# Attention, Fourier mixing and a two-layer network in one kernel: new token groups, weight sums moved from GpSimd to VectorE, buffers kept double for one more batch

## The chip, the cores and the metric

The kernel runs on one core of one Trainium2 chip. The metric is the device time of one execution in microseconds (us); the time of a kernel is the median over its runs. The engines are called by the names of the profile: PE is TensorE (matrix products; PEld its weight loads), DVE is VectorE, ACT is ScalarE, POOL is GpSimd, SP is SyncE, which here only issues DMAs. Each engine works its own instructions strictly in the order in which they stand, and waits on semaphores for the others.

## What is computed

For 8 batches of 448 tokens, 12 heads of 64:

```python
scores = scale * np.matmul(q, k.transpose(0, 1, 3, 2))
attn = np.maximum(scores, 0.0) ** 2 / S
x = attn @ v                                   # heads side by side: 768 channels
mixed = np.real(np.fft.fft(np.fft.fft(x, axis=1), axis=2))
u = x + mixed                                  # over tokens, then over channels
un = (u - mean(u)) / np.sqrt(var(u) + 1e-6)    # per token
out = u + np.maximum(un @ w_ch1, 0.0) @ w_ch2  # 768 -> 3072 -> 768
```

Attention and the Fourier mixing need a whole batch. The two layers of the network work on any token by itself.

## The kernel before, in words

**Batches and groups.** Attention and mixing go by batch, b = 0 to 7. The network goes by groups of tokens that run across batch borders; `GT` (L171) holds the borders. There are nine groups, called 0 to 8 here: 384, 512, 256, 512, 512, 512, 256, 512 and 128 tokens.

**A batch.** `load_group` (L305) fetches q, k and v of four heads at a time from POOL; three such loads make a batch. q and k have two buffers each, of which `home` (L301) picks one: both are used in turn up to load 10, from load 11 on only one. `turning` (L400) copies q and k on DVE (L412) and transposes them by DMA from SP (L424). `attention` (L525) computes scores on PE (L588, three pieces of a head pair at a time), takes relu on ACT (L612) and squares on DVE (L618) into one of nine buffers `sq` (six from batch 3 on), and multiplies by v on PE (L573). `fold` (L465) scales the result, and forms sums and differences for the Fourier step on DVE (L474 to L511). `mix` (L1019) does the channel transform on PE (L1035), `mix_rows` (L858) the token transform (L866), then adds x on POOL and DVE into `u` (L886, L888), computes mean and variance (L901), and writes the normalised rows `un` on POOL (L918). u and un go to DRAM (L940 from SP, L943 from POOL as an indirect store). `u` and `un` have two sets of buffers up to batch 2, and one from batch 3 on (`side`, L629; L906 and L916): with one set the second half of the rows waits until the first half is stored.

**A group.** `turn_un` (L966) transposes a group's rows from DRAM into the tile `unT` by DMA from SP (L972). It waits for the stores of un and for a free unT buffer: there are two, `unT0` and `unT1`, but `unT0` is given up after group 0 to hold weight sums, so all later groups share `unT1`. `ffn` (L1177) then does the first layer (L1222, 144 products whatever the group's size, as wide as the group), relu on ACT (L1200), and the second layer. Groups in `PLAIN` (0, 1 and 8) do the second layer with 24 products for each 128 tokens and half of the 768 channels (L1255). All others take two blocks of 128 tokens as a `Pair` (L1265) and use Strassen's scheme on 16 of the 24 hidden blocks: 88 products (L1312) where the plain way has 96, with extra sums of relu outputs on DVE (L1293 to L1305) and with sums of `w_ch2`'s blocks. Each product's result is added to u on DVE (L1209) and stored (L1168).

**The weight sums.** `weight_sums` (L1093) makes four sets of eight blocks, 128 partitions x 384, once, on POOL (L1104): T3, T2, T4 and T1. They are put into tiles that are free by then: `unT0`, `uA` and `u1A`, two `sq` and `qn0`, `kn0`. T1 overwrites a block of w_ch2 in place, once group 1, a plain one, has read it (`w2_free`). Group 8, plain again, needs that block, so `load_left` (L1119) loads it a second time at the end of attention.

**Who sets the order.** The engines' programs are written out by a planner (`Streams`, L63). Each part of the work is a stream that asks for an engine with an estimated duration, dependences and buffers; the planner always takes the request that can start first, and so fixes the order of the instructions on every engine. A wrong estimate makes an engine wait with work behind it. Attention is held back so that it stays ahead of the network by a fixed amount: PE may take the next scores of batch b when the network's progress, in batches, has reached b plus the batch's share done minus `LEAD` (L1396, L559).

Of the kernel before, what the change touches and what calls it, by code (L numbers as in the profile page):

```python
# [142 lines left out]
def kernel(  # L143
# [9 lines left out]
    nc = tc.nc  # L153
# [17 lines left out]
    GT = [0, 384, 896, 1152, 1664, 2176, 2688, 2944, 3456, B * S]  # L171
# [129 lines left out]
    def home(i):  # L301

        return (i - NG) % 2 if i < 4 * NG - 1 else 1
# [96 lines left out]
    def turning():  # L400

        for b in range(B):
            for g in range(NG):
# [5 lines left out]
                for x in range(2):  # L409
# [115 lines left out]
    def attention(b):  # L525
# [3 lines left out]
        if b == 3:  # L529
# [3 lines left out]
        room = NSQ if b < 3 else NSQ - 3  # L533
# [95 lines left out]
    def side(b, ch):  # L629

        return ch if b < 3 else 1
# [226 lines left out]
    def mix_rows(b, ch, pcs):  # L858
# [47 lines left out]
        e = yield need("DVE", 0.3, [e3 + LATENCY["ACT"]], [BUN[ch if b < 3 else 0]])  # L906
# [5 lines left out]
        for i, u in enumerate(us):  # L912
# [3 lines left out]
            un = work.tile([128, D], BF16, name="un", tag=f"un{2 * (ch if b < 3 else 0) + i}", bufs=1)  # L916
# [164 lines left out]
    PLAIN = (0, 1, NGR - 1)  # L1081
# [3 lines left out]
    sums, left, left_ready = [Cell() for _ in range(5)], [], Cell()  # L1085
    ffn_begun = [Cell() for _ in range(NGR)]
    unt_left, w2_free, attended = Cell(), Cell(), Cell()
# [5 lines left out]
    def weight_sums():  # L1093

        def slots(tag, count, deps):
            yield need("POOL", 0.0, deps)
            t = work.tile([128, count, DH], BF16, name="wsum", tag=tag, bufs=1)
            return [t[:, i] for i in range(count)]

        def each(n, outs, xs, ys, op, deps):  # L1100
            T[n] = outs
            for i in range(KP):
                e = yield need("POOL", 1.3, deps)
                nc.gpsimd.tensor_tensor(outs[i], xs[i], ys[i], op=op)  # L1104
            sums[n].t = e + LATENCY["POOL"]

        t3 = yield from slots("unT0", 8, [unt_left] + w2_ready)
        b11, b12, b21, b22 = ([w2(2 * i + k, hf) for i in range(KP)] for k in range(2) for hf in range(2))
        yield from each(3, t3, b22, b12, ALU.subtract, [])
        t2 = yield from slots("uA", 4, u_left)  # L1110
        t2 += yield from slots("u1A", 4, u_left)
        yield from each(2, t2, t3, b11, ALU.add, [sums[3]])
        t4 = []
        for tag, dep in ((f"sq{NSQ - 2}", sq_left), (f"sq{NSQ - 1}", sq_left), ("qn0", qk_left), ("kn0", qk_left)):
            t4 += yield from slots(tag, 2, [dep])
        yield from each(4, t4, b21, t2, ALU.subtract, [sums[2]])
        yield from each(1, b12, b12, b11, ALU.subtract, [w2_free, sums[3]])

    def load_left():  # L1119

        yield need("POOL", 0.0, [attended])
        for i in range(0, KP, 2):
            e = yield need("POOL", 0.85)
            t = work.tile([128, 2, DH], BF16, name="left", tag=f"sq{i // 2}", bufs=1)
            nc.gpsimd.dma_start(out=t, in_=moe_w_ch2[2 * i * 128:(2 * i + 4) * 128, DH:D].rearrange(
                "(j p) d -> p j d", p=128)[:, 0::2])
            left.extend([t[:, 0], t[:, 1]])
        left_ready.t = sch.dma(e, KP * 128 * DH * 4, 360e3, "sw")
# [48 lines left out]
    def ffn(b):  # L1177
# [38 lines left out]
        for j in range(0, JC, JN):  # L1216
            hf, jj = divmod(j, JC // 2)
            e = yield need("PE", 6 * JN * mm(N), [w1_ready[hf]], [BF])
# [14 lines left out]
        if b == 0:  # L1233
# [12 lines left out]
        for c in range(NC):  # L1246
            for hf in range(2):
                for jq in range(4):
                    e = yield need("PE", 6 * mm(DH), ht[6 * jq:6 * jq + 6] + [w2_ready[jq]]
# [197 lines left out]
```

## Time and profile before

| what | value |
|---|---|
| median of three runs | 627.71 us (625.6 to 630.43) |
| the profiled execution | 628.35 us, of which the span of the trace 626.6 us |
| PE busy | 591.0 us (94%), 4118 products |
| DVE busy | 401.7 us (64%) |
| ACT busy | 293.2 us (47%) |
| POOL busy | 188.2 us (30%) |
| first layer, L1222, 512 wide | 165.9 us busy, 720 products |
| second layer, L1312 and L1255 | 1264 products of 384 columns |
| POOL weight sums, L1104 | 32 instructions, the four sets between 89.8 and 225.2 us |

A row of the timeline gives start, duration, engine, line, operation, output<-input, shape and count; in brackets stands the idle time of the engine before it and what ended it. Products overlap in the array, so the mean duration of one (387 ns at 512 columns) is longer than the step from one to the next: 24 of them in 5.29 us make a step of 220 ns. Steps, not durations, are what a chain of products costs. A row of windows gives busy time of each engine in a stretch of the span, and the clock that PE was granted there (1.00 is full).

### The profile page before, as it was taken

The numbers are of one execution on the slowest core, as the hardware profiler recorded it, in microseconds if no ns is written. First come the engines' busy times: TensorE is split into PE (matmuls) and PEld (weight loads), VectorE is DVE, ScalarE is ACT, GpSimd is POOL, SyncE is SP. The second block draws the span as 40 slices with busy tenths as digits, with TensorE's granted clock in tenths as the row PEclk, the third lists the DMA queues.
The fourth block names the chain that finished last, engine by engine and source line by source line (L and its number), as shares of the span: only waits on it lengthen the run. The fifth ranks groups of instructions, "written<-read, shape, count | busy, mean of one in ns | idle before, by whom it ended". The sixth has DMA issues, their size and how long they took to land.

```text
span 626.6 us, 10716 instructions
## 1 busy us (share of the span) xinstructions
PE 591.0 (94%) x4118; PEld 331.3 (53%) x4118; DVE 401.7 (64%) x886; ACT 293.2 (47%) x427; POOL 188.2 (30%) x236
## 2 busy tenths in 40 slices
PE   8999999899999989579999999999999999699997
PEld 6565556544544566224555454554545577344675
DVE  6977787846599867726598565975687759101520
ACT  5867741767344325338523556345572442044001
POOL 8442227111389535201243015121161016100000
PEclk9999999999999889979999999999999999899999
DMA  9999999768859764756957985598445364600220
GB/s 130 208 207 229 217 183 179 148 78 146 141 152 174 129 118 135 124 78 91 158 168 144 134 122 156 137 191 139 103 137 126 66 128 143 167 22 0 79 86 26
DMA packets 134484, 83.04 MB, mean 133 GB/s; under 512 B 77473, under 2 KB 129601, under 8 KB 134433
## 3 DMA queue, kind: packets, MB, share of 16 engines
q0 software_dynamic: 41408, 34.86, 35.0%
q1 hardware_dynamic: 93024, 47.50, 33.6%
q8 instruction: 32, 0.52, 0.3%
q14 instruction: 20, 0.16, 0.1%
HBM read 64.49 MB, written 26.69 MB: 146 GB/s over the span
## 4 chain that ended last, share of the span: by engine, by line
PE 71%; issue 10%; DVE 9%; DMA 3%; ACT 3%; POOL 2%; SPq 1%; POOLq 0%; DVEq 0%; ACTq 0%
PE psF L1222 33%; PE psF L1312 16%; PE psF L1255 7%; PE psF L573 5%; PE psS L588 5%; DVE sq L618 3%; DMA unT<-nbot 2%; PE psS L1035 2%; ACT sq L612 2%; PE psS L866 1%; SPq L972 1%; DVE o L1209 1%; DMA out_dram<-o 1%; DVE fold L497 1%; PE psS L665 1%
## 5 line engine op out<-in xcount | busy, mean ns | idle before, releaser
L1222 PE MATMUL psF<-unT,w 128*128 128x512 bf16 (+3 forms) x1296 | 231.9, 336 | 17.6 <-DMA unT<-nbot 15.8
L612 ACT ACTIVATE sq<-psS 112x896 bf16<-112x896 f32 x192 | 164.4, 916 | 115.4 <-PE psS L588 115.2
L1222 PEld LDWEIGHTS <-w 128*128 128x128 bf16 x1296 | 118.7, 99 | 121.8 <-issue 17.9
L1200 ACT ACTIVATE hT<-psF 128x512 bf16<-128x512 f32 (+1 forms) x162 | 95.5, 590 | 152.0 <-PE psF L1222 150.8
L618 DVE TENSOR_TENSOR sq<-sq 112x896 bf16<-112x896 bf16 x192 | 131.4, 699 | 35.5 <-ACT sq L612 34.5
L1312 PE MATMUL psF<-w,hT 128*128 128x384 bf16 x560 | 96.0, 326 | 0.0
L1312 PEld LDWEIGHTS <-hT 128*128 128x128 bf16 x720 | 69.6, 98 | 49.1 <-issue 3.7
L1209 DVE TENSOR_TENSOR o<-psF,o 128x384 f32<-128x384 f32 x96 | 53.0, 552 | 65.7 <-PE psF L1312 50.3
L1255 PE MATMUL psF<-w,hT 128*128 128x384 bf16 x376 | 66.2, 329 | 0.5 <-DVE o L1209 0.5
L588 PE MATMUL psS<-qkT 64*112 64x448 bf16 x384 | 52.9, 369 | 2.1 <-ACT sq L612 0.9
L319 POOL DMA_DIRECT2D vn<-in_v_dram x24 | 17.2, 718 | 118.7 <-PE psF L573 99.1
L1255 PEld LDWEIGHTS <-hT 128*128 128x128 bf16 x384 | 36.7, 98 | 28.1 <-issue 5.3
L573 PE MATMUL psF<-sq,vn 112*64 112x448 bf16 x384 | 46.4, 360 | 4.5 <-DVE o L1209 2.3
L474 DVE TENSOR_SCALAR xT<-psF 128x224 bf16<-128x224 f32 x48 | 18.7, 389 | 43.1 <-PE psF L573 42.9
L918 POOL TENSOR_SCALAR un<-u,rstd,nmr 128x768 bf16<-128x768 f32 (+1 forms) x24 | 28.3, 1186 | 54.4 <-DVE nmr L910 54.3
L588 PEld LDWEIGHTS <-qkT 64*112 64x112 bf16 x384 | 20.9, 126 | 27.8 <-issue 21.6
L573 PEld LDWEIGHTS <-vn 112*64 112x64 bf16 x384 | 18.3, 109 | 27.9 <-issue 19.6
L1293 DVE TENSOR_TENSOR s<-hT 128x768 bf16<-128x768 bf16 (+1 forms) x20 | 8.8, 438 | 33.3 <-ACT hT L1200 32.6
L1312 PE MATMUL psF<-wsum,hT 128*128 128x384 bf16 x160 | 29.3, 326 | 0.1
L901 DVE BATCH_NORM_STATS2 stats<-u 128x6 f32<-128x384 f32 (+1 forms) x56 | 28.4, 540 | 0.0
L319 POOL DMA_DIRECT2D qn<-in_q_dram x21 | 15.1, 717 | 44.0 <-DVE qkr L412 36.2
L943 POOL DMA_INDIRECT ubot<-u,back x16 | 16.7, 1046 | 24.0 <-ACT hT L1200 19.8
(139 smaller groups left out, 542.0 us busy)
## 6 DMA issues: line engine op xcount, KB each, us to landing
out_dram<-o SPq DMA_DIRECT2D x56, 192.0 KB, 1.9
vn<-in_v_dram POOLq DMA_DIRECT2D x24, 224.0 KB, 4.9
qn<-in_q_dram POOLq DMA_DIRECT2D x21, 224.0 KB, 4.9
kn<-in_k_dram POOLq DMA_DIRECT2D x21, 224.0 KB, 5.6
w<-in_moe_w_ch_dram POOLq DMA_DIRECT2D x12, 384.0 KB, 13.5
w<-in_moe_w_ch_dram POOLq DMA_DIRECT2D x4, 1152.0 KB, 22.6
utop<-u SPq DMA_DIRECT2D x8, 384.0 KB, 2.7
o<-utop SPq DMA_DIRECT2D x16, 192.0 KB, 4.2
```

Of the source, the lines that this page charges most:

```text
L319: nc.gpsimd.dma_start(out=t, in_=src[b, hs].rearrange("h (p j) d -> p h (j d)", j=4))
L573: nc.tensor.matmul(av[h * Dh:(h + 1) * Dh, 0:S], lhsT=vn[:, c, h0 + h, :], rhs=sq[:, h, :], start=(c == 0), stop=(c == 3))
L588: nc.tensor.matmul(sc[:R, h, 0:S].rearrange("k (c q) -> k c q", c=4), lhsT=kT[ps, m % 2, c, :], rhs=qT[ps, m % 2], start=True, stop=True)
L612: nc.scalar.activation(r, sc[:R, :, 0:S], AF.Relu)
L618: nc.vector.tensor_tensor(r, r, r, op=ALU.mult)
L901: nc.vector.bn_stats(stats[:n, hf, :], u[:n, hf * (D // 2):(hf + 1) * (D // 2)])
L918: nc.gpsimd.tensor_scalar(un[:n], u[:n], rstd[:n, i:i + 1], nmr[:n, i:i + 1], op0=ALU.mult, op1=ALU.add)
L1200: nc.scalar.activation(hs, ps, AF.Relu)
L1209: nc.vector.tensor_tensor(o, pc[:, 0:DH], o, op=ALU.add)
L1222: nc.tensor.matmul(ph[:, i * N:(i + 1) * N], lhsT=w1_sb[m][hf][:, (jj + i) * 128:(jj + i + 1) * 128], rhs=unT[:, m, 0:N], start=(m == 0), ...
L1255: nc.tensor.matmul(pc[:, 0:DH], lhsT=h[:, j, c * 128:(c + 1) * 128], rhs=left[j // 2] if swap else w2(j, hf), start=(j == 0), stop=(j == J ...
L1312: nc.tensor.matmul(pc[:, 0:n], lhsT=lhs[i], rhs=rhs[i], start=(start and i == 0), stop=(i == k - 1), skip_group_check=True)
```

## The change

- The groups become 384, 512, 384, 512, 256, 512, 512 and 512 tokens: eight, called 0 to 7. Plain are 0, 1 and 2; the nine pairs of groups 3 to 7 use the seven products.
- Group 2 is transposed into `unT0`, so groups 1 and 2 have a buffer each; `unT0` is given up to the sums after group 2's first layer.
- The weight sums go from POOL to DVE, up to three blocks in one instruction (15 instructions), and T1 is made after group 2. The second load of w_ch2's block and its stream go.
- q/k buffers stay double up to load 11, and `u`, `un` and the nine `sq` buffers up to batch 3, one batch longer.
- `LEAD` goes from 2.3 to 2.6 batches.

```diff
-    GT = [0, 384, 896, 1152, 1664, 2176, 2688, 2944, 3456, B * S]
+    GT = [0, 384, 896, 1280, 1792, 2048, 2560, 3072, B * S]
...
-        return (i - NG) % 2 if i < 4 * NG - 1 else 1
+        return (i - NG) % 2 if i < 4 * NG else 1
...
-                    if b * NG + g != 4 * NG - 3:
+                    if b * NG + g != 4 * NG - 1:
                         BQ[x][home(b * NG + g)].free.append(e)
...
-        if b == 3:
+        if b == 4:
             yield need("ACT", 0.0, [], [BSQ] * 3)
...
-        room = NSQ if b < 3 else NSQ - 3
+        room = NSQ if b < 4 else NSQ - 3
...
-        attended.t = max(t for t, _ in sq_ids)
...
-        return ch if b < 3 else 1
+        return ch if b < 4 else 1
...
-        e = yield need("DVE", 0.3, [e3 + LATENCY["ACT"]], [BUN[ch if b < 3 else 0]])
+        e = yield need("DVE", 0.3, [e3 + LATENCY["ACT"]], [BUN[ch if b < 4 else 0]])
...
-            un = work.tile([128, D], BF16, name="un", tag=f"un{2 * (ch if b < 3 else 0) + i}", bufs=1)
+            un = work.tile([128, D], BF16, name="un", tag=f"un{2 * (ch if b < 4 else 0) + i}", bufs=1)
...
-            if b == 2 and ch == 0:
+            if b == 3 and ch == 0:
                 u_left[i].t = t
...
-            if b == 2 and ch == 1:
+            if b == 3 and ch == 1:
                 un_left.t = n_stored[b][3].t
             else:
-                BUN[0].free.append(n_stored[b][2 * ch + 1].t)
+                BUN[ch if b < 3 else 0].free.append(n_stored[b][2 * ch + 1].t)
...
-                g = work.tile([128, MC, 512], BF16, name="unT", tag="unT1", bufs=1)
+                g = work.tile([128, MC, 512], BF16, name="unT", tag=f"unT{int(len(groups) != 2)}", bufs=1)
...
-    PLAIN = (0, 1, NGR - 1)
+    PLAIN = (0, 1, 2)
...
-        def each(n, outs, xs, ys, op, deps):
-            T[n] = outs
-            for i in range(KP):
-                e = yield need("POOL", 1.3, deps)
-                nc.gpsimd.tensor_tensor(outs[i], xs[i], ys[i], op=op)
-            sums[n].t = e + LATENCY["POOL"]
...
+        def several(n, outs, x, y, op, deps):
+
+            def blocks(z, i0, i1):
+                if isinstance(z, tuple):
+                    k, hf = z
+                    j0 = 2 * i0 + k
+                    return w2_sb[j0 // 6][:, j0 % 6:j0 % 6 + 2 * (i1 - i0) - 1:2, hf * DH:(hf + 1) * DH]
+                return z[i0][0][:, z[i0][1]:z[i0][1] + i1 - i0]
+
+            i0 = 0
+            for i1 in range(1, KP + 1):
+                whole = [z for z in (outs, x, y) if not isinstance(z, tuple)]
+                if i1 < KP and i1 % 3 and all(z[i1][0] is z[i0][0] for z in whole):
+                    continue
+                e = yield need("DVE", dve2((i1 - i0) * DH), deps)
+                a, b, c = (blocks(z, i0, i1) for z in (outs, x, y))
+                nc.vector.tensor_tensor(a, b, c, op=op)
+                i0 = i1
...
+            sums[n].t = e + LATENCY["DVE"]
...
+        yield from several(3, t3, b22, b12, ALU.subtract, [])
...
+        yield from several(2, t2, t3, b11, ALU.add, [])
...
+        yield from several(4, t4, b21, t2, ALU.subtract, [])
+        yield from several(1, b12, b12, b11, ALU.subtract, [w2_free])
-
-    def load_left():
-
-        yield need("POOL", 0.0, [attended])
-        for i in range(0, KP, 2):
-            e = yield need("POOL", 0.85)
-            t = work.tile([128, 2, DH], BF16, name="left", tag=f"sq{i // 2}", bufs=1)
-            nc.gpsimd.dma_start(out=t, in_=moe_w_ch2[2 * i * 128:(2 * i + 4) * 128, DH:D].rearrange(
...
-        if b == 0:
+        if b == 2:
             unt_left.t = e
...
-        if b == 1:
+        if b == 2:
             w2_free.t = e + LATENCY["PE"]
...
-    LEAD = 2.3
+    LEAD = 2.6
...
-        sch.add(load_left(), (6, 6))
```

More of the change, by code (lines that the diff above doesn't have):

```diff
@@ L1084 @@
     T = [None] * 5
-    sums, left, left_ready = [Cell() for _ in range(5)], [], Cell()
+    sums = [Cell() for _ in range(5)]
     ffn_begun = [Cell() for _ in range(NGR)]
-    unt_left, w2_free, attended = Cell(), Cell(), Cell()
+    unt_left, w2_free = Cell(), Cell()
     def w2(j, hf):
@@ L1093, in weight_sums, with home @@
     def weight_sums():
-        def slots(tag, count, deps):
-            yield need("POOL", 0.0, deps)
+        def home(tag, count, deps):
+            yield need("DVE", 0.0, deps)
             t = work.tile([128, count, DH], BF16, name="wsum", tag=tag, bufs=1)
-            return [t[:, i] for i in range(count)]
-        def each(n, outs, xs, ys, op, deps):
-            T[n] = outs
-            for i in range(KP):
-                e = yield need("POOL", 1.3, deps)
-                nc.gpsimd.tensor_tensor(outs[i], xs[i], ys[i], op=op)
-            sums[n].t = e + LATENCY["POOL"]
@@ L1107, in weight_sums @@
[L1107 to L1112, printed above, removed]
+            return [(t, i) for i in range(count)]
+        def several(n, outs, x, y, op, deps):
[14 more added lines that the diff above has]
+                i0 = i1
+            T[n] = [w2(2 * i + outs[0], outs[1]) if isinstance(outs, tuple) else outs[i][0][:, outs[i][1]]
+                    for i in range(KP)]
+            sums[n].t = e + LATENCY["DVE"]
@@ L1116, in weight_sums @@
[L1116 to L1128 removed]
+            t4 += yield from home(tag, 2, [dep])
```

14 lines of the change are left out of this document (7 added, 7 removed).

## The prediction

> **What bounds the kernel now.** I read the page's slices first, then the waits, then the chain of work that ended last, then the timeline around each gap of PE. Groups and batches are counted from 0.
>
> The slices say that PE is the bound nearly everywhere, so only its gaps and its clock can be won:
>
> ```profile
> PE   8999999899999989579999999999999999699997
> PEclk9999999999999889979999999999999999899999
> ```
>
> A slice is 15.7 us. The digits 5, 7 and 6 in PE's row, and the 8s in the clock's row, are three places: 204 to 235, 251 to 282 and 533 to 548 us. The waits (who waited for what: total, times, longest) name two causes:
>
> ```profile
> PE psF L1222 <- DMA unT<-nbot: 15.8, 3, 10.4
> ...
> PE psS L1035 <- DVE fold L511: 2.9, 1, 2.9
> ...
> PE psF L573 <- DVE o L1209: 2.3, 1, 2.3
> ```
>
> The timeline of PE has them in place, the idle time in brackets:
>
> ```profile
> 182.77 0.38 PE L573 MATMUL psF<-sq,vn 112*64 112x448 bf16 x2 [1.00 <-DVE sq L618]
> 184.31 3.08 PE L1255 MATMUL psF<-w,hT 128*128 128x384 bf16 x18 [0.45 <-DVE o L1209]
> 204.94 1.19 PE L573 MATMUL psF<-sq,vn 112*64 112x448 bf16 x8 [2.34 <-DVE o L1209]
> 226.45 0.34 PE L1035 MATMUL psS<-chan,fold 128*128 128x193 bf16 x1 [2.88 <-DVE fold L511]
> 270.87 5.48 PE L1222 MATMUL psF<-unT,w 128*128 128x512 bf16 x18 [10.35 <-DMA unT<-nbot]
> 350.57 1.46 PE L1222 MATMUL psF<-unT,w 128*128 128x512 bf16 x6 [0.53 <-DMA unT<-nbot]
> 544.24 34.20 PE L1222 MATMUL psF<-unT,w 128*128 128x512 bf16 x144 [4.97 <-DMA unT<-nbot]
> ```
>
> Three of these wait for a group's transposed rows (groups 3, 4 and 7). The first four wait for DVE, and the timeline of DVE and POOL around the third shows what held it:
>
> ```profile
> 197.08 5.90 DVE L618 TENSOR_TENSOR sq<-sq 112x896 bf16<-112x896 bf16 x1
> 197.25 5.24 POOL L1104 TENSOR_TENSOR wsum<-w,wsum 128x384 bf16<-128x384 bf16 x6
> ...
> 203.09 0.61 DVE L618 TENSOR_TENSOR sq<-sq 112x896 bf16<-112x896 bf16 x1
> ```
>
> The same square takes 0.61 us alone and 5.90 us while six of POOL's weight sums run. A fold at 221.45 takes 3.90 us beside four sums (221.70, 3.50 us). So a run of POOL's sums holds DVE, and PE behind it.
>
> A gap costs more than its length. In the windows of 2 us (PE busy first, then PEld, DVE, ACT, POOL, granted clock, DMA share, GB/s) the clock is half for some time after it:
>
> ```profile
> 206.00:208.00 2.00, 2.00 (x11) 0.79 (x10) 1.02 (x3) 1.28 (x2) 1.56 (x2) 0.50 0.89 173
> 272.00:274.00 2.00, 2.00 (x6) 0.70 (x5) 0.00 (x0) 0.29 (x1) 0.00 (x0) 0.56 0.03 3
> 548.00:550.00 2.00, 2.00 (x6) 0.73 (x5) 0.00 (x0) 0.45 (x1) 0.00 (x0) 0.50 0.62 176
> ```
>
> The chain gives the step of a product, and what the half clock cost (start, duration, count):
>
> ```profile
> 270.87 5.48 PE psF L1222 x18
> 277.93 3.99 PE psF L1222 x18
> 293.77 5.29 PE psF L1222 x24
> 314.54 3.92 PE psF L1312 x24
> 544.24 34.20 PE psF L1222 x144
> ```
>
> Steps: first layer at 512 columns 5.29/24 = 0.220 us, second layer 3.92/24 = 0.163. After the long gap 18 products took 5.48 instead of 3.99 us (1.5 lost); after the last, 144 took 34.20 instead of 31.75 (2.4 lost).
>
> **The change part by part.**
>
> *Products.* The first layer's columns stay 144 x 3584, and its step goes with the width (144 products of 128 columns take 8.04 us in the chain, a quarter of 31.75), so merging groups gives nothing. The second layer goes from 1264 to 10 x 48 = 480 plain and 9 x 88 = 792 others, 1272: 8 more, 8 x 0.163 = +1.3 us on PE, exposed. The second load of w_ch2 (four DMAs, 5.9 us to landing, at 509.8) was hidden; its going gives 0.
>
> *Waits for unT.* I took the order of PE's instructions in both programs and summed their steps between the last token-transform product (L866) of a batch and the first product (L1222) of the group that needs it. That is the cover for u, un, its store, and the transpose. (Other steps by the same division: values 0.110 us, scores 0.118, channel transform 0.083, token transform 0.166, first layer 0.167 at 384 columns and 0.111 at 256.) An example: batch 7 to group 7 has 72 products of group 6's first layer, 8.0, and its pair, 88 x 0.163 = 14.3, before; 120 x 0.220 = 26.4 and two pairs, 28.7, after.
>
> Before: batch 3 to group 3 25.5 us, batch 4 to group 4 38.1, batch 5 to group 5 49.0, batch 6 to group 6 53.8, batch 7 to group 7 22.2. What was needed, from the timeline: 233.8 to 270.9 = 37 us for batch 3, 310.7 to 350.6 = 40 for batch 4, 516.8 to 544.2 = 27 for batch 7. All three that waited had less cover than that.
>
> After: batch 2 to group 2 41.5 us, batch 3 to group 3 55.2, batch 4 to group 4 73.3, batch 5 to group 5 47.3, batch 6 to group 6 62.0, batch 7 to group 7 55.1. Every one is over 40. So the gaps of 10.35, 0.53 and 4.97 us go, with 1.5 and 2.4 of half clock: -19.75 us. Late next is the unT buffer: group 5 can be transposed only after group 4's first layer, 18.2 us before it starts. Its three transposes take about 3 x 1.3 us on SP's queue and 4.3 to land (medians of L972), 8 us; what SP must finish first (store of the last un rows of batch 5, a transpose of batch 6's x) is due earlier. Slack 10 us. Group 2's last transpose stands on SP behind stores of five of group 1's eight results; counted so, it lands some 8 us ahead.
>
> *Sums off POOL.* The four DVE waits are 1.00 + 0.45 + 2.34 + 2.88 = 6.7 us. The half clock behind them: windows 204 to 210 lose 0.2 + 1.0 + 0.5, windows 226 to 230 0.8 + 0.7, together 3.2. All go: -9.9 us. Bounds: -6.7, if the clock falls for another reason, and -11.6, if the 1.73 us wait for ACT's unT copy at 124.64, 25 us after the first set, goes too.
>
> *Sums onto DVE.* 15 instructions, 12,288 elements a partition. L1293 takes 554 ns for 768 elements and 284 for 256, so 0.527 ns an element and 0.15 us each: 6.5 + 2.2 = 8.7 us of DVE. They stand between the squares of batch 4. Summing rows of DVE's order, DVE has 46 us of work between the channel transforms of batches 3 and 4, PE 57: hidden, 0 us. If that cover fails, all 8.7 show; the nearest strided row, L1305 (652 against 554 ns), makes it 10.3. Nothing is gained below 0, since DVE only gets more. T1 and T4 are ready some 40 us before group 3's second layer. Queued behind the sums on DVE are squares and adds; PE waits for those.
>
> *Double buffers, LEAD, loads.* Batch 3's scores start 3 us of PE work after batch 2's channel transform instead of 13. They give the longer cover above and are not counted again. q, k and v loads need the same number of issues on POOL, whose queue loses 32 sums of 0.9 us in front of them.
>
> *Sum.* 626.6 + 1.3 - 19.75 - 9.9 = 598.2 us of span. New small gaps: the denser stages put 12 squares of 0.92 us and 24 relus of 0.49 beside 31.7 us of PE in group 2, 18 and 24 of 0.60 in group 3, where ACT is at some 80%; before, the windows give 232.75 us of busy PE from 305 to 544, so 239 - 232.75 - 4.97 = 1.3 us of small gaps. Bounds 0 and 5; I take 1.5, as that stage is the nearest. Span 599.7, and 1.75 around it as in the profiled run (628.35 - 626.6); that run lies 0.64 above the median: 600.8, said as 601 us.
>
> *Floor.* From batch 2's channel transform (160.5) to the last product (622.9) the steps of all products sum to 427.2 us, and it took 462.4: 35.2 us are lost there, of which I take back 29.65. If all goes, and the 1.73 us as well: 601 - 5.5 - 1.5 - 1.7 = 592 us.
>
> **The rivals.**
>
> R1, DVE becomes the bound in batch 4's stretch: the sums stand in front of squares in order, and PE waits as it did for POOL. For: any long DVE row stopped PE before. Against: single sums are at most 0.76 us, not 5.9, and DVE has 11 us spare. Price 10.3: 611 us.
>
> R2, the wait for unT moves to group 2 or 5: SP is held by a store in front of the transposes. For: SP waited 94.8 us for L1209 in all, and the transposes are queued behind stores. Against: slack of 8 and 10 us. Price as at group 3 before, 10.35 + 1.5: 613 us.
>
> R3, slower: attention starves. From batch 4 on q and k have one buffer, and a group of heads needs POOL issue 1.4, landing 5.6, copy 0.95, two transposes 2.6 and landing 3.1: 13.7 us in a ring. In the changed order batch 4 leaves 55.6/3 = 18.5 us a group, batch 3, with two buffers, 46/3 = 15.3. If the ring takes more than the pace, PE stops each time; from 2 us in each of 18 groups of heads it decides, 36 us: 637 us. Against: no PE wait for q or k before, at 40/3 = 13.4 us in batch 3.
>
> R4, the change doesn't do what it says: the DVE rows were long for another reason and the new order waits elsewhere as much: 628 us.
>
> R5: the half clock at 206 and 226 us is not of the short gaps in front of it and stays: 601 + 3.2 = 604 us. Against: it begins right behind them, and the clock is 1.00 for most of the rest. [...]
>
> **How the numbers follow.** Forecast 0.62 (592 to 607 by itself: the floor, and above 3.2 for the sums' lesser gain and 3.5 for small gaps), R1 0.11, R2 0.12, R5 0.06, R3 0.05, R4 0.04. The time is the forecast's, 601. The range leaves out R3 and R4: 592 to 614. About 1% is what a measurement of this kernel can tell from no change. Faster is forecast, R1, R2 and R5, 0.91; the same is R4, 0.04; slower is R3, 0.05.
>
> **What would show it.** Right: no wait of PE for unT over 1 us in the changed profile; PE's slices 13 to 17 and 34 (the first is 0) at 9; no L618 above 2 us; L1115 (the sums) 15 rows of DVE, 8 to 10 us; clock at 1.00 from 180 us to the end. R1: PE waits naming DVE between L1115 rows. R2: a PE wait for unT at group 2 or 5. R3: waits of L588 for qkT. Wrong above all if a gap of over 5 us opens at a place where I count cover.

## The result, and the profile after

The changed kernel takes 600.21 us (median of four runs, 599.02 to 601.21), the kernel before 629.07 beside it (four runs, 625.6 to 630.54): a ratio of 0.955, 95% interval 0.950 to 0.960. The forecast was 601 us, with a range from 592 to 614. The profiled execution after took 599.02 us, of which the span is 597.2.

The page's slices after (14.9 us each), to be laid beside those of before:

```profile
PE   8999999989999999999989999999999999999997
PEclk9999999999999999999999999999999999999999
```

The three holes of PE's row and the 8s of the clock's are gone. PE is busy for 98% of the span. The 8 near the middle, slice 20, is one of the gaps that are left. From 100 us to the end the timeline of PE has two waits of over half a microsecond:

```profile
124.25 2.75 PE L1225 MATMUL psF<-unT,w 128*128 128x512 bf16 x11 [1.74 <-ACT unT L839]
...
307.88 2.76 PE L1225 MATMUL psF<-unT,w 128*128 128x512 bf16 x11 [2.00 <-DVE xT L478]
```

The first stood there before as well (1.73 at 124.64). The second is new. No wait names a transposed tile `unT<-nbot`, which were three of the seven rows shown of before. The timeline of DVE shows where the new one comes from:

```profile
306.79 0.43 DVE L412 COPY qkr<-kn 112x1024 bf16<-112x1024 bf16 x1 [3.31 <-DMA qkT<-qkr]
307.13 0.38 DVE L474 TENSOR_SCALAR xT<-psF 128x224 bf16<-128x224 f32 x1
307.44 0.39 DVE L478 TENSOR_SCALAR xT<-psF 128x224 bf16<-128x224 f32 x1
```

DVE stood 3.31 us in front of a copy into `qkr`, which has a single buffer and whose transposition had not ended. The two rows behind it empty the bank that PE wants next. The products they read (L573, from 302.82 on) had ended at 303.77, yet the two rows ran only at 307.13 and 307.44, behind the copy, as the order has them. PE's wait names the last of them, L478; the cause is two rows up, in front of a copy that PE is not waiting for.

The sums (L1115) are 15 rows of DVE, at 242.2 to 254.3 us and at 276.2 to 277.5, some 8.7 us together. The squares after, then before (count, then shortest, median and longest row in ns):

```profile
L618 DVE TENSOR_TENSOR sq<-sq x192: 571/619/1332, 10.4 to 463.8; 112x896 bf16<-112x896 bf16 x192
```

```profile
L618 DVE TENSOR_TENSOR sq<-sq x192: 571/620/5901, 10.4 to 505.7; 112x896 bf16<-112x896 bf16 x192
```

The median is the same and the longest falls from 5.9 to 1.3 us: no DVE row is held any more.

Where the 29.4 us of span went: the steps of PE's instructions, summed over the order of both programs, are 576.4 before and 577.7 after (+1.3). From the start of batch 2's channel transform to the end of the last product PE takes 433.4 us after (159.99 to 593.43), of which 428.5 are steps: it loses about 4.9 us there, against 35.2 before (-30.3). The rest, -0.4, is in front of it, where this channel transform starts at 159.99 instead of 160.38.

### The profile page after: what moved, and what is told of

Read it like the earlier page. It is cut to its first block, busy times and chain, and to the rows that moved or that the text cites. A ratio compares the mean times of both kernels' runs of the same rounds, so it can differ in the third digit from the quotient of the medians.

```text
span 597.2 us, 10407 instructions
## 1 busy us (share of the span) xinstructions
PE 583.0 (98%) x3962; PEld 321.8 (54%) x3982; DVE 390.7 (65%) x889; ACT 292.5 (49%) x433; POOL 156.4 (26%) x200
## 4 chain that ended last, share of the span: by engine, by line
PE 85%; DVE 6%; ACT 3%; SPq 2%; DMA 2%; issue 1%; POOL 0%; DVEq 0%; ACTq 0%; POOLq 0%
PE psF L1225 32%; PE psF L1312 22%; PE psF L1256 13%; PE psF L573 6%; PE psS L588 6%; PE psS L1034 2%; ACT sq L612 2%; DVE sq L618 2%; PE psS L865 1%; SPq L1167 1%; DMA qkT<-qkr 1%; PE psS L664 1%; DVE stats L900 1%; PE psS L1009 1%; DVE u L887 0%
## 5 line engine op out<-in xcount | busy, mean ns | idle before, releaser
L1225 PE MATMUL psF<-unT,w 128*128 128x512 bf16 (+2 forms) x1132 | 226.2, 352 | 5.4 <-DVE xT L478 2.0
L1225 PEld LDWEIGHTS <-w 128*128 128x128 bf16 x1152 | 109.4, 98 | 114.0 <-issue 13.9
L1203 ACT ACTIVATE hT<-psF 128x512 bf16<-128x512 f32 (+1 forms) x168 | 96.7, 576 | 127.9 <-PE psF L1225 124.7
L618 DVE TENSOR_TENSOR sq<-sq 112x896 bf16<-112x896 bf16 x192 | 121.9, 651 | 37.5 <-ACT sq L612 36.8
L1212 DVE TENSOR_TENSOR o<-psF,o 128x384 f32<-128x384 f32 x92 | 50.9, 554 | 70.6 <-PE psF L1312 67.6
L1312 PEld LDWEIGHTS <-hT 128*128 128x128 bf16 x648 | 62.9, 98 | 43.6 <-issue 2.1
L1312 PE MATMUL psF<-w,hT 128*128 128x384 bf16 x504 | 85.7, 326 | 0.0
L1256 PE MATMUL psF<-w,hT 128*128 128x384 bf16 x480 | 82.1, 326 | 0.0
L1256 PEld LDWEIGHTS <-hT 128*128 128x128 bf16 x480 | 45.5, 98 | 34.0 <-issue 5.7
L319 POOL DMA_DIRECT2D vn<-in_v_dram x24 | 17.3, 721 | 120.0 <-PE psF L573 108.9
L573 PE MATMUL psF<-sq,vn 112*64 112x448 bf16 x384 | 45.5, 358 | 0.5 <-ACT hT L1203 0.5
L885 POOL TENSOR_TENSOR u<-tp,xn 128x385 f32<-128x385 f32 (+1 forms) x14 | 13.2, 942 | 97.3 <-DVE tp L874 89.8
L917 POOL TENSOR_SCALAR un<-u,rstd,nmr 128x768 bf16<-128x768 f32 (+1 forms) x24 | 28.7, 1199 | 28.9 <-DVE nmr L909 26.3
L573 PEld LDWEIGHTS <-vn 112*64 112x64 bf16 x384 | 17.8, 109 | 22.7 <-issue 14.1
L319 POOL DMA_DIRECT2D qn<-in_q_dram x21 | 15.2, 721 | 50.3 <-DVE qkr L412 41.8
L1312 PE MATMUL psF<-wsum,hT 128*128 128x384 bf16 x144 | 26.4, 326 | 0.0
```

Of the source, the lines that this page charges most:

```text
L319: nc.gpsimd.dma_start(out=t, in_=src[b, hs].rearrange("h (p j) d -> p h (j d)", j=4))
L573: nc.tensor.matmul(av[h * Dh:(h + 1) * Dh, 0:S], lhsT=vn[:, c, h0 + h, :], rhs=sq[:, h, :], start=(c == 0), stop=(c == 3))
L618: nc.vector.tensor_tensor(r, r, r, op=ALU.mult)
L917: nc.gpsimd.tensor_scalar(un[:n], u[:n], rstd[:n, i:i + 1], nmr[:n, i:i + 1], op0=ALU.mult, op1=ALU.add)
L1203: nc.scalar.activation(hs, ps, AF.Relu)
L1212: nc.vector.tensor_tensor(o, pc[:, 0:DH], o, op=ALU.add)
```

## The experiments

The theory to test is the prediction's: two causes that have nothing to do with each other, rows of unT that come late and DVE rows that POOL's sums hold. Its rivals are that one of the two changes does it all, and that the gain comes from the wider buffers and `LEAD`.

The first four runs share their runs of the kernel before (626.81 us, median of seven).

**Sums back on POOL.** All else as changed:

```diff
-                e = yield need("DVE", dve2((i1 - i0) * DH), deps)
+                e = yield need("POOL", 1.3, deps)
...
-                nc.vector.tensor_tensor(a, b, c, op=op)
+                nc.gpsimd.tensor_tensor(a, b, c, op=op)
```

> The changed kernel with its weight sums on GpSimd again, one block of 384 each (32 instructions). Theory (a run of POOL's sums holds DVE, and PE waits behind it): squares or folds on DVE of 2 us and more beside runs of three or four sums, PE waits naming DVE of 3 to 7 us in all with half clock after them; 600 plus 6.7 to 9.9, 607 to 610 us. Rival (the long DVE rows of the kernel before had another cause, and the gain is all cover for the transposed rows): no such rows, 600 us. Since the sums stand in other places here, fewer of them may meet a square that PE waits for: at 603 or below the theory of the hold stands, but its price depends on the place.

Measured: 616.68 us (615.4 to 617.11), ratio to before 0.983 (0.981 to 0.986). That is 16.5 us above the changed kernel (18.1 between the two profiled executions), well over the 9.9 that the prediction took for this part. The timeline of all engines in the stretch:

```profile
255.35 0.73 POOL L319 DMA_DIRECT2D vn<-in_v_dram  x1 [0.41 <-issue]
256.06 6.26 DVE L497 TENSOR_TENSOR fold<-xT 128x225 bf16<-128x225 bf16 x1
256.08 6.09 POOL L1113 TENSOR_TENSOR wsum<-wsum,w 128x384 bf16<-128x384 bf16 x7
...
263.99 1.59 PE L573 MATMUL psF<-sq,vn 112*64 112x448 bf16 x8 [4.81 <-DVE o L1210]
...
273.39 0.70 POOL L319 DMA_DIRECT2D vn<-in_v_dram  x1 [1.37 <-PE psF L573]
...
273.85 7.37 DVE L497 TENSOR_TENSOR fold<-xT 128x225 bf16<-128x225 bf16 x1
...
274.10 0.92 POOL L1113 TENSOR_TENSOR wsum<-wsum,w 128x384 bf16<-128x384 bf16 x1
...
274.98 6.10 POOL L1113 TENSOR_TENSOR wsum<-w,wsum 128x384 bf16<-128x384 bf16 x7
...
282.32 0.34 PE L1034 MATMUL psS<-chan,fold 128*128 128x193 bf16 x1 [5.22 <-DVE fold L511]
```

A fold of 0.28 us (L497's median) takes 6.26 and 7.37, to within 0.2 us of the end of POOL's run each time. Before, the two long holds were 5.90 and 3.90; here POOL finds seven and eight sums ready in one go. The two waits of PE are 10.0 us, and the half clock behind them costs an estimated 4.6 (the windows have it from 264.2 to 267.6 and, with PE at work again from 282.3, to 288.0). Another 1.7 is a half clock at 124 to 128 us of this execution, long before these sums. So the mechanism is the predicted one; the size was of the old order.

**Only the sums moved.** The kernel before with the sums' functions of the changed one:

```diff
-        yield from each(3, t3, b22, b12, ALU.subtract, [])
+        yield from several(3, t3, b22, b12, ALU.subtract, [])
```

> The kernel before with nothing changed but the weight sums, which go to DVE in up to three blocks at a time. Theory: the four PE waits for DVE between 182 and 227 us and the half clock behind them go, 9.9 us, and the waits for unT of groups 3, 4 and 7 stay: 628 - 9.9 = 618 us (617 to 621). Group 3's cover is 24.8 us by the order, as before, so its wait of about 10 us stays. Rival one (no hold): 628 us. Rival two (the sums on DVE lie on the path): 618 + 8.7 = 627 us, with PE waits naming the sums.

Measured: 620.02 us (618.31 to 623.95), ratio 0.987 (0.985 to 0.990), so 6.8 us gained. PE's timeline keeps the waits for unT, and two of the three rows have nearly the old length (the profiled execution is the slowest of the five):

```profile
261.66 0.61 PE L1237 MATMUL psF<-unT,w 128*128 128x512 bf16 x1 [9.04 <-DMA unT<-nbot]
...
345.92 0.38 PE L1237 MATMUL psF<-unT,w 128*128 128x512 bf16 x1 [2.85 <-DMA unT<-nbot]
...
541.51 0.59 PE L1237 MATMUL psF<-unT,w 128*128 128x512 bf16 x1 [4.81 <-DMA unT<-nbot]
```

Group 3 starts 9.2 us earlier than before, group 4 only 4.65: the middle wait grew from 0.53 to 2.85. Part of what one cause gives back is taken by the other.

**Only the groups changed.** The new groups, `PLAIN` and unT tiles, with POOL's sums, single buffers as before and `LEAD` of 2.3:

```diff
-        room = NSQ if b < 4 else NSQ - 3
+        room = NSQ if b < 3 else NSQ - 3
...
-                nc.vector.tensor_tensor(a, b, c, op=op)
+                nc.gpsimd.tensor_tensor(a, b, c, op=op)
...
-    LEAD = 2.6
+    LEAD = 2.3
```

> The new groups, plain groups and unT buffers alone: weight sums on GpSimd, q, k, u, un and sq double only up to batch 2, LEAD 2.3, all as in the kernel before. Cover by the order, batch to group: 42.6, 50.3, 73.3, 39.3, 53.9 and 52.5 us for groups 2 to 7. Theory (the groups alone give the cover): no wait for unT over 1 us but perhaps at group 5 (39.3 against a need of 37 to 40); the DVE hold stays with the POOL sums: 628 + 1.3 - 19.75 = 609 us, 607 to 613. Rival (cover comes from the longer double buffers and LEAD): waits for unT of 5 to 10 us stay, 615 to 620 us.

Measured: 616.1 us (615.31 to 616.24), ratio 0.983 (0.980 to 0.985), 10.7 us gained. PE has no wait for unT at all, so the groups alone give the cover. But from 260 to 322 us it has 11.9 us of other waits (1.75, 2.66, 0.26, 5.23 and 1.97), against the 6.7 behind held DVE rows before; the longest, in the timeline:

```profile
278.21 0.71 POOL L319 DMA_DIRECT2D vn<-in_v_dram  x1 [2.21 <-PE psF L1254]
278.67 7.37 DVE L497 TENSOR_TENSOR fold<-xT 128x225 bf16<-128x225 bf16 x1
278.93 6.98 POOL L1113 TENSOR_TENSOR wsum<-w,wsum 128x384 bf16<-128x384 bf16 x8
...
287.15 0.34 PE L1034 MATMUL psS<-chan,fold 128*128 128x193 bf16 x1 [5.23 <-DVE fold L511]
```

The two parts alone gain 6.8 and 10.7, 17.5 in sum; together, with the wider buffers and `LEAD`, 26.6 to 28.9 (against 626.81 and 629.07). Without the wider buffers they still gain 23.5 (604.16 against 627.67, the run on single buffers below), so the sum of the parts is short of the whole by 6 us at least. Both rivals of a single cause fall. Between this run and the one with the sums back on POOL only buffers and `LEAD` differ: 616.1 and 616.68, so these two are worth nothing as long as POOL has the sums.

**The group of 256 last.** This takes group 4's cover away again (10.1 us of PE work by the same sum):

```diff
-    GT = [0, 384, 896, 1280, 1792, 2048, 2560, 3072, B * S]
+    GT = [0, 384, 896, 1280, 1792, 2304, 2816, 3328, B * S]
```

> The changed kernel with its group of 256 tokens moved from fifth to last place, all else equal; the summed steps of PE's products are the same, 577.7 us. Cover by the order: batch 2 to group 2 41.5 us, batch 3 to group 3 55.2, batch 5 to group 4 10.1, batch 6 to group 5 33.9, batch 7 to group 6 35.3. Theory (what counts is cover against a need of 27 to 40 us): a wait for unT of 17 to 30 us at group 4, 0 to 6 at groups 5 and 6, 1.5 to 2.4 of half clock after each: 600 + 25 + 2 = 627 us, 618 to 640. Rival (group 3's wait in the kernel before came from the single un buffer in batch 3 and the shared unT1, not from cover): no wait over 5 us, 600 to 605 us.

Measured: 612.36 us (610.95 to 612.62), ratio 0.976 (0.974 to 0.979). The wait comes where the cover went, but shorter than expected, and with the half clock behind it (timeline of PE, then a window of 2 us with its columns as in the prediction, the granted clock behind POOL):

```profile
367.49 0.61 PE L1225 MATMUL psF<-unT,w 128*128 128x512 bf16 x1 [9.39 <-DMA unT<-ntop]
```

```profile
368.00:370.00 2.00, 1.78 (x5) 0.50 (x4) 0.00 (x0) 0.00 (x0) 0.00 (x0) 0.50 0.84 189
```

From the end of batch 5's last token transform (346.95) to 367.49 are 20.5 us, less than the 27 to 40 of before. But it is not the same way. Batch 5 begins at token 2240 and group 4 now ends at 2304, so the group needs only the first 64 rows of this batch, a single transposition of `ntop`, where groups 3, 4 and 7 before need 320 or 384 rows, of `ntop` and of `nbot`. Even so, SP issued it only at 364.85, right behind the store of the second half's rows (364.42), though the first half's were stored from 355.80 on. In the kernel before, the second half's rows of batch 3 were written at 255.96, 7.9 us after POOL was free: DVE had the statistics for them from 251.57 on between squares and adds of the network, and the reciprocal at 255.50. SP then issued the transposition at 262.82 behind other transpositions.

**Single buffers, sums on DVE.**

```diff
-        return ch if b < 4 else 1
+        return ch if b < 3 else 1
```

> The changed kernel with single buffers one batch earlier, as in the kernel before (q and k, squares, u, un); cover of the transposed rows, summed over PE's order, 42.6, 47.6, 64.0, 32.7, 53.9 and 52.5 us for groups 2 to 7. The theory that the buffers do nothing by themselves while cover stays above the bare need of some 20 us expects no wait for unT and 600 us (598 to 603). The prediction's own need of 27 to 40 us expects a wait at group 5 (32.7): up to 7 us, 601 to 609. If single buffers hold the attention of batch 4 (ring of q and k), waits of scores show in batch 3's or 4's stretch and it takes over 606.

Measured: 604.16 us (603.71 to 605.11), ratio 0.961 (0.956 to 0.966; this run and the next beside 627.67, median of seven). My expectation of 600 was wrong, as its need of 20 us was that of 64 rows; the prediction's own need of 27 to 40 was right: group 5, with a cover of 32.7 for 320 rows, waits 1.24 us, in front of it PE waits 2.1 us for squares and relus, and the clock is half from 390.2 to 400.5:

```profile
396.31 0.61 PE L1225 MATMUL psF<-unT,w 128*128 128x512 bf16 x1 [1.24 <-DMA unT<-nbot]
```

```profile
398.00:400.00 2.00, 2.00 (x6) 0.75 (x5) 0.40 (x1) 0.60 (x1) 0.00 (x0) 0.50 1.26 248
```

Its un rows of the second half were scaled at 382, 24 us after the last token transform at 357.6, and SP issued `ntop`'s transposition at 387.53: 38.7 us in all. So the need is no constant: 27 to 40 us for 320 or 384 rows of a batch, as DVE's order and SP's queue leave it, and 20.5 for 64. Batch 5 has single buffers in every version here, so this spread is not the buffers'; what the wider ones change for group 5 is its cover (47.3 in the changed kernel). The wider buffers are worth some 4 us once the sums are off POOL, and none before.

**LEAD of 2.3.**

```diff
-    LEAD = 2.6
+    LEAD = 2.3
```

> The changed kernel with the old LEAD of 2.3: covers 41.5, 55.2, 72.6, 37.7, 49.0 and 47.2 us. The theory that LEAD only shifts cover that is ample anyway expects 600 us (598 to 603) and no wait for unT. The rival, that LEAD is what gives the cover, expects a wait at group 5 (37.7 against the prediction's need of 40) and 602 to 606.

Measured: 601.11 us (599.81 to 602.9), ratio 0.957 (0.952 to 0.962): not told apart from 600.21. Group 5, with 37.7 us of cover, waits for unT as the rival said, but 0.41 us; the wait at 308 us is 2.52 instead of 2.00.

```profile
390.66 1.46 PE L1225 MATMUL psF<-unT,w 128*128 128x512 bf16 x5 [0.41 <-DMA unT<-nbot]
```

So the need is again some 38 us.

**How a gap sets the clock.** Copies of a part of unT onto itself on DVE, in front of five steps of group 7's first layer:

```diff
+            k = PROBE.get(j, 0) if b == NGR - 1 else 0
+            for _ in range(k):
+                yield need("DVE", 0.3)
+                nc.vector.tensor_copy(unT[:, 0, 0:N], unT[:, 0, 0:N])
```

> The changed kernel with PE stopped five times on purpose in the first layer of group 7, by 2, 4, 6, 9 and 14 copies of a part of unT onto itself on DVE (the values stay); gaps of about 0.9, 1.4, 1.9, 2.7 and 4.1 us are estimated from DVE's copies (0.42 us for 1024 elements). The theory that a gap from about 2.3 us on halves the clock (rows of the kernel before: half behind 2.34 and 2.88 us, not behind 1.74; of the changed one: not behind 2.00) expects a clock of 1.00 behind the first three gaps and 0.5 for 3 us or more behind the last two. [...] The whole: 600.2 plus the gaps' 11 us plus 2 to 4 us, 613 to 616.

Measured: 608.69 us (one run). Gaps of 0.29, 1.89, 1.94 and 3.58 us (the shortest number of copies was hidden), and the clock is 1.00 behind each of them, behind the 3.58 too. Timeline of PE, then the window of 1 us behind the gap:

```profile
572.73 1.47 PE L1229 MATMUL psF<-unT,w 128*128 128x512 bf16 x6 [3.58 <-DVE unT L1225]
```

```profile
573.00:574.00 1.00, 1.00 (x6) 0.45 (x5) 0.00 (x0) 0.00 (x0) 0.00 (x0) 1.00 0.00 0
```

> The same with 8, 10, 7, 5 and 12 copies: gaps of about 2.5, 3.0, 2.2, 1.7 and 3.6 us. [...] The whole: 600.2 plus 13 plus 3 to 7 us, 616 to 620.

Measured: 616.51 us (one run). The clock is half behind gaps of 2.26 and 2.22 us, and full behind one of 2.92, as it was behind 3.58 above, so the length alone, from about 2.3 us on, does not decide here:

```profile
551.41 0.97 PE L1229 MATMUL psF<-unT,w 128*128 128x512 bf16 x3 [2.26 <-DVE unT L1225]
...
561.97 8.34 PE L1229 MATMUL psF<-unT,w 128*128 128x512 bf16 x29 [2.22 <-DVE unT L1225]
...
580.50 1.47 PE L1229 MATMUL psF<-unT,w 128*128 128x512 bf16 x6 [2.92 <-DVE unT L1225]
```

```profile
551.00:552.00 1.00, 0.59 (x3) 0.31 (x4) 0.32 (x2) 0.00 (x0) 0.00 (x0) 0.98 0.00 0
552.00:553.00 1.00, 0.78 (x3) 0.30 (x2) 0.00 (x0) 0.00 (x0) 0.00 (x0) 0.50 0.00 0
...
555.00:556.00 1.00, 1.00 (x5) 0.43 (x4) 0.00 (x0) 0.04 (x1) 0.00 (x0) 0.82 0.00 0
...
562.00:563.00 1.00, 1.00 (x3) 0.36 (x4) 0.85 (x2) 0.00 (x0) 0.00 (x0) 0.60 0.00 0
...
565.00:566.00 1.00, 1.00 (x4) 0.35 (x3) 0.00 (x0) 0.21 (x1) 0.00 (x0) 0.70 0.00 0
```

The rows above date the half clock: from 551.96 (0.98 is 0.04 of a microsecond at half) to 555.36, and from 562.2 to 565.6. Both last 3.4 us, and their starts lie 10.24 apart, three times 3.41. The kernel before shows the same step in windows of 0.1 us: the clock is half from 205.51 to 208.92, 225.99 to 229.41, 263.54 to 273.78 and 543.43 to 550.26, for one, one, three and two times 3.413 us, and the starts lie 20.48, 37.55 and 279.89 apart, 6, 11 and 82 times 3.413. So the half clock's dates fit a grid of 3.41 us in these two executions. In the squares of the grid ahead of these starts (548.55 to 551.96, 558.8 to 562.2) PE stood still for 2.26 and 2.2 us, 65% of them; in the squares ahead of 205.51 and 225.99 in the kernel before (202.10 to 205.51, 222.58 to 225.99) for 2.34 and 2.42 us, 69 and 71%. The gap of 2.92 lies across a border of the same grid (579.26), 1.68 us on one side and 1.24 on the other. In the run with the gap of 3.58 the grid can be dated too, by a half clock early in it, from 123.7 to 127.1 us:

```profile
123.00:124.00 1.00, 0.00 (x0) 0.00 (x0) 1.00 (x3) 1.00 (x2) 0.00 (x0) 0.85 1.03 198
...
127.00:128.00 1.00, 1.00 (x5) 0.39 (x4) 0.00 (x0) 0.60 (x1) 0.00 (x0) 0.94 0.47 97
```

Counted on from there in steps of 3.413 (a third of 10.24), borders lie at 560.6 and 570.8. The gap of 3.58 (569.15 to 572.73) is cut into 1.7 and 1.9 us, and the one of 1.94 lies in one square nearly whole; 55% of a square idle left the clock full there, where 65% in the other run did not. Idle time is not the whole measure, though: the square in front of 123.7, with values, scores and products of 97 columns in it, has only 1.6 us of idle time, 48%, and the half clock came. Most of it is the wait for ACT's unT copy at 124 us, which is in every version here, 1.73 or 1.74 us long: the clock was half behind it in six of the fourteen profiled executions (here from 123.7 to 127.1) and full in eight (1.00 from 120.2 to 127 us in the kernel before). The grid lies differently in each of the three executions dated here: counted back in steps of 3.413, its first border falls 0.71 us behind the start of the span in the kernel before, 0.8 in the run with the gap of 3.58 and 2.4 in the other. That may be what parts the four executions of the changed kernel, though that is not shown: two with a mean clock of 1.00 took 599.02 and 599.4 us, and those with 0.997 and 0.994 took 601.03 and 601.21.

**What holds DVE.** Behind the end of the changed kernel, blocks on dead memory: six sums on POOL as the kernel's, three DVE operations beside them, everything waited for in between.

```diff
+        for pk, dk in [(0, 0), (0, 1), (0, 2), (0, 3), (0, 4), (0, 5), (0, 6), (0, 7), (1, 0), (1, 2), (0, 0), (0, 5)]:
+            nc.vector.tensor_copy(A[:, 0, 0:384], A[:, 6, 512:896])
+            pool(pk)
+            for i in range(3):
+                dve_op(dk, i)
```

> The changed kernel, and behind its end twelve blocks on dead memory: in each, six sums of 384 (or six scalings) run on POOL while DVE does three operations of one kind: in-place squares of 896, sums of 225 of two inputs, copies of 1024, a maximum with zero of 896, fp32 sums of 384, adds of 384 from PSUM, a maximum from PSUM, fp32 copies of 384; last, squares and copies beside scalings on POOL, and two blocks again. The theory that a run of POOL's sums holds whatever DVE does next until the run ends expects the first DVE row of each block at 4 to 6 us, also where it reads PSUM. The rival, that only some kinds are held (DVE rows of bf16 alone, as the squares and folds in the traces so far; the adds from PSUM were never seen held), expects long rows in the bf16 blocks and 0.3 to 0.6 us in the blocks with fp32 or PSUM. A third, that the two engines take turns (as at 252 to 260 us in the run with the old buffers, where squares took 1.15 us each and POOL's sums 1.12), expects no row over 1.5 us. The time is 600 plus some 12 x 6.5 = 78 us, 670 to 690, and says nothing by itself.

Measured (683.97 us, one run): no hold in any block. The first block in the timeline, as an example:

```profile
609.42 3.10 DVE L1438 TENSOR_TENSOR bench<-bench 112x896 bf16<-112x896 bf16 x3
609.68 3.61 POOL L1433 TENSOR_TENSOR bench<-bench 128x384 bf16<-128x384 bf16 x3 [110.96 <-DVE bench L1455]
```

The first of the three squares starts before POOL and takes its usual 0.61 us; the two behind it take 1.33 each, and a sum 1.2 in place of 0.87: they take turns. Operations of DVE that read PSUM are not touched (three adds 1.73 us, and POOL's six sums keep their 5.24). The turns are the third theory of the expectation; what made the holds of the kernel was still open.

**Operations from PSUM in front,** so that POOL's run stands alone when DVE comes to SBUF:

```diff
+            for i in range(pre):
+                dve_op(6, i)
```

> The changed kernel with blocks behind its end again. In the bench before, DVE's first operation was already under way in SBUF when POOL's run of sums began, and the two took turns (DVE rows of 0.6 us took 1.0, POOL's sums 1.04 instead of 0.87). Here DVE first does one, two or four operations that read PSUM (0.55 us each), so that POOL's run stands alone when DVE's next operation in SBUF comes. The theory that a run of sums on POOL that has begun alone keeps DVE out until it ends expects the first such DVE row at 3 to 5 us with six sums on POOL, 1 to 2 us with three, and turns (1.0 us each) in the block without the PSUM operations. The rival, that the hold needs something else of the kernel's own surroundings (its DMA traffic, its operands), expects turns in all blocks, no row over 1.5 us. The time, 600 plus some 80 us, says nothing by itself.

Measured (687.19 us, one run): turns again everywhere, a square at most 1.35 us and a fold of 225 at most 1.00. My theory fell: it is not enough that POOL began alone.

**The issue of a load in front of the sums,** as in the kernel, where a v load stands right ahead of the held runs:

```diff
+                nc.gpsimd.dma_start(out=t, in_=v[0, 0:HG].rearrange("h (p j) d -> p h (j d)", j=4))
+            pool(0, 6)
```

> The changed kernel with blocks behind its end a third time. In the kernel before, each of the runs of sums that held DVE to its end came right behind the issue of a load on POOL (a v tile, 0.70 to 0.73 us), and transfers were under way; the two benches so far had neither, and DVE and POOL took turns in all 24 blocks. Here five blocks issue such a load in front of POOL's six sums, two have two loads of 0.8 MB on SP's queue beside them, four have both, the last none; DVE starts with none, one or two operations that read PSUM. The theory that the load's issue in front makes the hold expects a DVE row of 3 to 6 us in the first five blocks and in the four with both; the theory that traffic makes it expects it in the two with SP's loads and the four. If neither is the cause, turns everywhere, no row over 1.5 us, and what tells a hold from turns stays open.

Measured (691.67 us, one run): four holds, and the second block shows how they look:

```profile
615.44 0.73 POOL L1464 DMA_DIRECT2D benchv<-in_v_dram  x1
...
616.18 0.92 POOL L1433 TENSOR_TENSOR bench<-bench 128x384 bf16<-128x384 bf16 x1
616.36 5.54 DVE L1438 TENSOR_TENSOR bench<-bench 112x896 bf16<-112x896 bf16 x1
```

A square of 0.61 us takes 5.54, to the end of the six sums (5.23 us from 616.18, so none of them lost anything). Of nine blocks with a load, the four where POOL went from the issue into the sums without a wait, and DVE was not yet in SBUF, all hold (rows of 5.54, 4.76, 5.52 and 4.77). In three, POOL waited 0.1 to 1.2 us for DVE between issue and sums, and in two DVE was in SBUF first (in one of these POOL had waited too, its load being issued 110 us ahead): turns, five times. Loads on SP's queue change nothing: turns in both blocks that have only these. In every block without a load POOL waits for DVE's copy in front of its run, so no block tells the issue itself from the mere absence of a wait.

The rows of the kernels fit. From 170 to 330 us of the kernel before, of the two runs with the sums on POOL above, and of the next one, each DVE operation of over 2.2 us stands beside sums that begin within 0.05 us of the end of a transfer's issue on POOL (a load, L319, or an indirect store of u or un). The reverse does not hold: several runs behind an issue took turns (191.94 and 214.15 before, with squares of at most 1.83 and 1.33 us).

**POOL made to wait.** Sums on POOL, but ahead of each of the first 24 DVE sets one column of its output to zero:

```diff
+                if n != 1:
+                    w = yield need("DVE", 0.1, deps)
+                    nc.vector.memset(outs[i0][0][:, outs[i0][1], 0:1], 0.0)
+                    deps = [w + LATENCY["DVE"]]
                 e = yield need("POOL", 1.3, deps)
```

> The changed kernel with the sums on POOL again (32 instructions, as in the run of 616.7 us), but in front of each of the first 24 a DVE instruction sets one column of its output to zero (the sum overwrites it), so that POOL waits for DVE before each of these sums; the last 8 are as they were. In the benches, DVE was held to the end of a run only where POOL's sums came right behind a load's issue with no wait between; where POOL had waited in front of the run, they took turns in each of the blocks. The theory that this wait-free start makes the hold expects no DVE row over 2 us beside L1117 sums of the first 24, the PE waits of 4.8 and 5.2 us gone, and 601 to 606 us (turns still stretch DVE). The rival, that it is POOL's work itself that costs, however it starts, expects again long rows or as much loss in many small ones, and 612 to 617 us. In between, 606 to 612, both have a part.

Measured: 600.5 us (599.36 to 600.73), ratio 0.958 (0.953 to 0.962), against 616.68 for the same sums on the same engine without the wait, and 600.21 for the changed kernel. POOL does 33.5 us more than in the changed kernel (189.9 busy), and it costs nothing. PE's waits of 4.81 and 5.22 are gone. The 24 sums stand nearly where they stood, from 244.4 to 298.7 us (243.8 to 295.9 without the waits). One square beside them still took 2.21 us (at 287.61), a little over what I had expected at most: DVE's zero had been written by then, so that the sum began right behind an indirect store. The last eight sums, left as they were, show the other case in the same run:

```profile
308.34 0.74 POOL L319 DMA_DIRECT2D kn<-in_k_dram  x1
308.74 5.74 DVE L499 TENSOR_TENSOR fold<-xT 128x225 bf16<-128x225 bf16 x1
309.10 1.79 POOL L1117 TENSOR_TENSOR w<-w 128x384 bf16<-128x384 bf16 x2
```

They follow a load's issue with no wait and hold a fold for 5.74 us. PE is in a first layer then (L1227 from 307.64 us on), whose results go to ACT, and the run's 600.5 us show no price of it. No version measured beats the changed kernel by more than the runs scatter.

## Why the prediction was right

- **Products:** +1.3 us of steps, as worked out.
- **Waits for unT:** all three went with their half clock, and the groups alone do it. The step behind it, "what was needed" of 27 to 40 us, held for groups that need both halves of a batch: some 38 us at group 5 with `LEAD` of 2.3 and 38.7 with single buffers. It is not the need of every group: with the group of 256 last, group 4 needs 64 rows of its last batch and had them after 20.5 us, so that I expected 627 and 612.4 were measured. In the changed kernel every group's last batch gives it 256 rows or more, and every cover was above 40.
- **Sums off POOL:** the term of -9.9 was right for the kernel before, whose waits it added up. In the new order the same sums cost 16.5, as POOL finds longer runs ready. The change was forecast from the old order to the new, so the old price was the right one to take back; only the comparison with sums on POOL in the new order shows the other. "A run of POOL's sums holds DVE" was too wide: many runs take turns, and none that began with a wait held DVE here.
- **Sums onto DVE:** 8.7 us forecast, 8.7 found, and PE waits for DVE at no place between them. R1 is out.
- **R2 and R3:** PE waits for unT neither at group 2 nor at 5, and for `qkT` nowhere behind the first batch. With 32.7 us of cover R2 comes true at group 5 (single buffers, 1.24 us): its place was right.
- **R5:** in the profiled execution the clock is 1.00 to the last product, so the half clock at 206 and 226 did belong to the gaps in front, 2.34 and 2.88 us long.
- **Small gaps:** this term was mis-sized. The sum left 35.2 - 29.65 + 1.5 = 7.05 us of loss behind batch 2's channel transform; 4.9 were found, of which 2.00 are the wait behind `qkr`, which I had not named. The difference of some 2.15, with the 0.4 in front of it, is the 2.5 us by which the span fell short of 599.7. That the median came within 0.8 us of 601 is partly luck: it lies 1.2 above the profiled execution, where the forecast put it 0.64 below.
- **Buffers and LEAD:** they were to give the longer cover and nothing besides. The buffers do: without them group 5's cover is 32.7 instead of 47.3, and the kernel takes 604.16. `LEAD` adds nothing that can be told from noise (601.11 without it), though group 5 then just waits.

## What to carry to other kernels

Take a cover from the order of the critical engine, but take the need from a case that waits for as much of the data: 64 rows of a batch and 320 took 20.5 and 37 to 39 us while attention ran beside them. Two causes of waits on one chain can hide each other: each alone gave 6.8 and 10.7 us, both 23.5, and more with the wider buffers, so an edit that gives little by itself may be worth a second look beside the other one. Where POOL and DVE share work, look first at what stands in front of POOL's run; moving the work away was not needed, one wait in front of each of 24 sums did as much (600.5 us against 600.21).

## What the hardware showed that I had not expected

- Beside sums on POOL a DVE operation in SBUF either takes turns with them (a square up to 1.35 us in the blocks and 1.83 in the kernel before, in place of 0.61, a sum up to 1.3 in place of 0.87) or is held until the run ends (up to 7.37 us for a fold of 0.28). The holds came only behind a transfer's issue with no wait on POOL between, and operations that read PSUM were free of both (three adds 1.73 us beside six sums of 5.24). Whether the issue decides or only the missing wait, why the start of a run matters, and why some such runs still take turns, stays open.
- Equal gaps of PE cost unequally: 2.2 us of idle gave 3.4 us of half clock, and 2.92 us none: by the dates of the half clock, the first lay whole in one square of a grid of 3.41 us, the other across a border (1.68 and 1.24 us). The wait of 1.73 us at 124 us gave it in six executions of fourteen.
